# A fused attention and gated feed-forward kernel: two of the second layer's seven products split into seven smaller ones, with their sums on GpSimd, and results stored 32 rows at a time

## The chip, the cores and the metric

The kernel runs on one core of one Trainium2 chip. Such a core has five engines that run their own streams of instructions and meet only at semaphores: TensorE (PE in the profile; its weight loads are PEld), VectorE (DVE), ScalarE (ACT), GpSimd (POOL), and SyncE (SP), which here only issues transfers. TensorE writes to PSUM, the others work on SBUF, VectorE and ScalarE on PSUM too. Transfers to and from the device's memory run on 16 DMA engines. The metric is the device time of one execution in microseconds.

## The reference

Everything is float32. For each of 8 batches and 8 heads, with 576 rows of 64 columns:

```python
kv = np.einsum('bhsd,bhse->bhde', k, v)
out = np.einsum('bhsd,bhde->bhse', q, kv)
rms = np.sqrt(np.mean(out * out, axis=-1, keepdims=True) + 1e-06)
attn = out / rms * g_norm
```

The heads of one row are then put beside each other: `x` has 4608 rows and 512 columns, and goes through a gated feed-forward block with `w_gate` and `w_val` of 512 x 1536 and `w_out` of 1536 x 512:

```python
gate = 1.0 / (1.0 + np.exp(-(x @ w_gate)))
result = (gate * (x @ w_val)) @ w_out
```

The weights come as float64 and are converted on the chip.

## The kernel before

**Chunks.** The 4608 rows are worked on in nine chunks `c` of 512 rows (`G`), 0 to 8. A chunk goes through a first layer (`x` times the two wide weights, sigmoid, product: 12 tiles `gv` of 128 features by 512 rows) and a second layer (`gv` times `w_out`). Chunk 0 is computed plainly, while weights arrive and the attention of batches 0 and 1 is done. From chunk 1 on both layers use a scheme of Strassen's kind (Winograd's form): two by two blocks are multiplied with seven products in place of eight, at the price of sums of blocks. In the first layer one of those seven is itself split into seven again, with matmuls of 128 columns (`small`).

**The first layer** (`first_layer_fast`) runs over six pairs of features `f`. For each it issues TensorE's products in a fixed order, VectorE additions that collect them from PSUM, ScalarE copies and sigmoids in tiles `sg` (four buffers), and on GpSimd the sums of the next pair's weights (`w_sum`, `w_sums2`). After each pair VectorE forms the sums of `gv` that the second layer wants: `s12` and `s4` (`h_sum`, `h_sums`). The last pair of a chunk also issues the weight sums for the first pair of the next.

**The second layer** (`second_layer_fast`) takes two groups `g` of 2 x 128 rows. For each it runs seven products of six matmuls of 256 columns (line 870), in PSUM banks that it takes from a queue of five (`take`, `give`), and gathers the results in two `sg` tiles: `o2` for the rows of tile `2 + g`, `o1` for those of tile `g`. `t2w` are sums of blocks of `w_out`, formed once, during chunk 1. When both tiles of a group are complete they are stored. The order of the seven is: `gv` low times `b[1,1]`, `s12` times `t2w[2]`, `gv` high times `b[2,1]`, `gv` low times `t2w[3]`, `s12` times `t2w[1]`, `gv` high times `t2w[4]`, `s4` times `b[2,2]`. A matmul call of float32 is two instructions in the profile, so a product shows as x12.

**Order.** Nothing is reordered by a planner: every engine gets its instructions in the order in which the program writes them. What isn't part of the layers is put into a queue `fill`, and `slot()` takes one step out of it: seven times for each pair of features in the first layer, twice for each product in the second, so 42 and 28 times a chunk. In chunks 1 to 6, `feed(c + 1)` provides the attention steps of batch `c + 1`: transposes of q on VectorE (`turn`), k^T v on TensorE (`kv_mm`) and its copies on ScalarE (`kv_copies`), then, for two pairs of heads at a time (`two_pairs`), q times k^T v on TensorE, square and root on ScalarE, sums, scaling and transposes on VectorE, and transfers of the transposed result into the next chunk's `xT` through SP. Steps called `idle` do nothing but take a slot. After them come the sums of the next chunk's rows (`x_sums`, eight VectorE operations).

**Transfers.** SP issues nearly all of them, in order: k and v of the batch after next (`load_late`, at the end of a second layer, into the 21 buffers that `gv`, `s12` and `s4` also rotate through), q after the second transpose of a pair, the transfers into `xT`, and the stores. From batch 2 on, the rows of `x` lie in an order in which 32 rows of a tile are rows of the output six apart; `store` (line 487 on) writes one, two or three such groups in one DMA. Only the last two stores, of half a tile each, also use ScalarE's queue.

Of the kernel before, what the change touches and what calls it, by code (L numbers as in the profile page):

```python
# [20 lines left out]
def kernel(  # L21
# [11 lines left out]
    nc = tc.nc  # L33
# [71 lines left out]
    def load_late(b):  # L105


        if b >= B:
            return
        mains = {}  # L110
        for n in range(NHP):
            for name, src in (("k", k), ("v", v)):
                mains[n, name] = t = hp.tile([P, G], FP32, tag="gv", name="kv")
                nc.sync.dma_start(out=t.rearrange("p (h c) -> p h c", h=2),
                                  in_=src[b, 2 * n:2 * n + 2, 0:S4].rearrange("h (p j) d -> p h (j d)", j=NK4))
        rest = hp.tile([P, G], FP32, tag="gv", name="kv")
        for i, src in enumerate((k, v)):
            for r in range(2):
                nc.sync.dma_start(out=rest[PH * r:PH * r + PH, GH * i:GH * i + GH].rearrange("p (h d) -> p h d", d=HD),
                                  in_=src[b, NHP * r:NHP * r + NHP, S4:S].rearrange("h p d -> p h d"))  # L120
        kv_late[b] = mains, rest
# [219 lines left out]
    def feed(b):  # L341
# [96 lines left out]
        def turns_of(n):  # L438
            return [(DVE, lambda n=n, e=e: turn(n, e)) for e in range(2)]
# [2 lines left out]
        steps = turns_of(n0)  # L442

        if b > 2:
            steps += [(PE, idle)] * 4
        steps.append((PE, kv_mm))
        for i in range(2 * NC):
            for rs in ((0, 1), (2,)):
# [2 lines left out]
        u, *rest = two_pairs(n0)  # L451
        steps += turns_of(n0 + 1) + [u] + rest[:1] + [(PE, idle)] * (3 if b > 2 else 0) + turns_of(n0 + 2) + rest[1:]

        steps += [(PE, idle)] + turns_of(n0 + 3) + [(PE, idle)] * (4 if b > 2 else 0)
        return steps + two_pairs(n0 + 2) + [(PE, idle)] * 4

    def idle():
# [20 lines left out]
        return gv[c, f]  # L478

    def sg_tile():  # L480
        return sb.tile([P, G], FP32, tag="sg", name="sg", bufs=4)

    def store(c, t, ot, cols=slice(0, DM), queues=(nc.sync,)):

        r0 = i = 0
        while r0 < P:
            b, s = divmod(G * c + P * t + r0, S)
            rows = out[S * b:S * b + S, cols]
            if b < 2:
                j, p = divmod(s, NP)  # L490
                n = min(P - r0, NP - p)
                queues[i % len(queues)].dma_start(out=rows.rearrange("(p j) d -> j p d", j=NJ)[j, p:p + n],
                                                  in_=ot[r0:r0 + n, cols])
            else:
                half, c0 = divmod(s, S // 2)
                r, c0 = divmod(c0, XC)
                n = min(P - r0, XC - c0)
                queues[i % len(queues)].dma_start(
                    out=rows.rearrange("(r p g i) d -> i r g p d", p=QB, g=JH, i=2)[half, r, c0 // QB:(c0 + n) // QB],
                    in_=ot[r0:r0 + n, cols])  # L500
            r0 += n
            i += 1
# [28 lines left out]
    def give(i):  # L531
        free.append(i)
# [190 lines left out]
    def first_layer_fast(c):  # L723
        s, a, s2, ax = sx[c], quarters(c), sx2[c], quarters(c)[1, 2]

        def product(ps, wt, xs, new):
            for m in range(NK):
                nc.tensor.matmul(ps, wt[:, m, :], xs[:, m, :], start=(new and m == 0), stop=(m == NK - 1),  # L728
                                 skip_group_check=True)

        def small(ps, wt, xs, new):
            nc.tensor.matmul(ps, wt, xs, start=new, stop=True, skip_group_check=True)  # L732


        def p1(d):
            d["ia"], d["pa"] = take()
            product(d["pa"], d["bg"][:, 0:NK], a[1, 1], True)
            d["u"] = d["sg"] = sg_tile()
            nc.scalar.copy(out=d["sg"][:, h2], in_=d["pa"])  # L739

# [34 lines left out]
        for f in range(NF2):  # L775
# [3 lines left out]
            ones, twos = one["bg"], two["bg"]  # L779

            p1(one)
            p1(two)
            slot()


            g1, g2 = one["sg"], two["sg"]
            i_d = free[2]
            del free[2]
            pd = bank(i_d)
            small(pd[:, q1], ones[:, NK], ax[:, 0, q1], True)  # L790
            nc.scalar.copy(out=g1[:, q1], in_=pd[:, q1])
            small(one["pa"][:, q1], ones[:, NK + 1], ax[:, 1, q1], False)
            p6(one)
            small(pd[:, q1], tw2[2], s2[:, 1], False)
# [54 lines left out]
    def h_sums(c, f):  # L849
# [5 lines left out]
        tt(out=one[:, h2], in0=one[:, h1], in1=one[:, h2], op=ALU.subtract)  # L855
        tt(out=s4[c, f], in0=two[:, h1], in1=s[:, h2], op=ALU.subtract)

    def second_layer_fast(c):
        b = {(j, n): w2[:, NF2 * (j - 1):NF2 * j, DH * (n - 1):DH * n] for j in (1, 2) for n in (1, 2)}
        d1, d2 = slice(0, DH), slice(DH, DM)  # L860
        for g in range(2):
            t1, t2 = slice(P * g, P * g + P), slice(GH + P * g, GH + P * g + P)
            (i_a, pa), (i_b, pb) = (take() for _ in range(2))

            last = (c, g) == (NG - 1, 1)
            parts = [slice(0, DH // 2), slice(DH // 2, DH)] if last else [slice(0, DH)]

            def product(ps, hs, ws, new):
# [37 lines left out]
                    store(c, g, o1, y, (nc.sync, nc.scalar))  # L906
            if not last:
                store(c, g, o1)
            if g == 1:
                load_late(c + 2)  # L910

    def sums_of(c):
        if c < NG:
# [33 lines left out]
    for c in range(1, NG):  # L947
        if c + 1 < B:
            steps = feed(c + 1)
            if c == 1:  # L950

                i = 4
                while w2_sums:
                    steps.insert(i, (DVE, w2_sums.popleft()))
                    i += 3
            spread(steps, (1, 2, 3, 4, 5) if c == 1 else (2, 3, 4, 5))
        first_layer_fast(c)
        sums_of(c + 1)
        second_layer_fast(c)
        flush()  # L960


# [28 lines left out]
```

## Time and profile before

| what | value |
|---|---|
| median of 10 runs | 1076.39 us (1075.49 to 1079.07) |
| the profiled execution | 1075.69 us, span 1073.9 us, TensorE clock 0.998 |
| first layer, chunks 2 to 6 (first to last matmul) | 76.6 to 76.9 us |
| second layer, chunks 2 to 6 | 38.5 us |
| first and second layer, chunk 7 (no attention beside them) | 71.7 and 36.4 us |
| from the last matmul's stretch to the end | 8.0 us |

The span reaches from the first to the last instruction of the profiled execution. "Idle" of an engine is named after what ended it. A matmul's recorded duration includes time in which the next one has begun, so TensorE's rate is read from the starts. The tables by stretches give, for each engine, busy microseconds and (x) the number of instructions.

### The profile page before, as it was taken

To read this page: it belongs to the slowest core of one execution; us is meant where nothing else is said; L and a number is where in the kernel's file an instruction comes from. 1 tells how busy PE (TensorE), PEld (TensorE's weight loads), DVE (VectorE), ACT (ScalarE), POOL (GpSimd) and SP (SyncE) were. 2 spreads that over 40 slices of the span, in tenths; PEclk is the share of its full clock that TensorE was granted. 3 is DMA by queue.
4 is the path that set the end of the run, shared out by engine and by line. 5 is a ranking of instruction groups with operands and counts; after the bars stand their busy time and mean duration, and the time that the engine had idled before them with its cause. 6 is when DMAs were issued, how large, how long until landed. Compare 5 with 4: busy or idle time off the path is not lost.

```text
span 1073.9 us, 19464 instructions
## 1 busy us (share of the span) xinstructions
PE 1062.8 (99%) x7514; PEld 883.0 (82%) x7514; DVE 712.0 (66%) x1461; ACT 308.8 (29%) x737; POOL 442.1 (41%) x630
## 2 busy tenths in 40 slices
PE   9999999999999999999999999999999999999996
PEld 8544448888888888888888888888888888888886
DVE  4897767894579547863778357945786388628841
ACT  4654323331243114320423134312431122112210
POOL 0000036870367216640666046713663077307700
PEclk9999999999999999999999999999999999999999
DMA  9944710002400141012301140014001200010001
GB/s 266 247 157 157 244 31 20 24 18 59 119 12 15 44 128 33 12 35 64 98 23 35 43 119 13 25 46 137 13 12 27 58 2 1 2 38 2 1 1 40
DMA packets 69115, 64.96 MB, mean 60 GB/s; under 512 B 23712, under 2 KB 63008, under 8 KB 69024
## 3 DMA queue, kind: packets, MB, share of 16 engines
q1 hardware_dynamic: 68768, 63.69, 21.2%
q8 instruction: 60, 0.98, 0.4%
q14 instruction: 31, 0.25, 0.1%
q10 hardware_dynamic: 256, 0.03, 0.1%
HBM read 47.19 MB, written 9.44 MB: 53 GB/s over the span
## 4 chain that ended last, share of the span: by engine, by line
PE 97%; DMA 1%; DVE 1%; SPq 0%; issue 0%; DVEq 0%
PE mm L728 46%; PE mm L870 27%; PE mm L732 7%; PE mm L556 7%; PE mm L653 4%; PE at L395 2%; PE at L354 1%; DMA v<-in_v_dram 1%; PE at L556 1%; PE two L261 0%; PE two L291 0%; PE two L318 0%; PE two L272 0%; DMA g_col<-in_g_norm_dram 0%; PE at L360 0%; PE mm L634 0%
## 5 line engine op out<-in xcount | busy, mean ns | idle before, releaser
L720 POOL TENSOR_TENSOR tw<-gv 128x256 f32<-128x256 f32 x192 | 156.1, 823 | 231.6 <-DVE w L202 144.5
L728 PE MATMUL mm<-xT,tw 128*128 128x256 f32 x768 | 198.4, 381 | 0.0
L728 PE MATMUL mm<-sx,tw 128*128 128x256 f32 x768 | 197.4, 380 | 0.0
L802 POOL TENSOR_TENSOR sg<-sg 128x256 f32<-128x256 f32 x48 | 35.6, 742 | 341.5 <-ACT sg L801 341.3
L720 POOL TENSOR_TENSOR tw<-gv,tw 128x256 f32<-128x256 f32 x192 | 154.9, 826 | 0.0
L728 PEld LDWEIGHTS mm<-xT,tw 128*128 128x128 f32 x768 | 137.3, 190 | 17.4 <-issue 2.8
L728 PEld LDWEIGHTS mm<-sx,tw 128*128 128x128 f32 x768 | 134.9, 191 | 12.4
L773 DVE TENSOR_TENSOR gv<-gv,sg 128x256 f32<-128x256 f32 x192 | 108.4, 584 | 0.0
L728 PE MATMUL mm<-sx,gv 128*128 128x256 f32 x384 | 91.2, 380 | 0.0
L728 PE MATMUL mm<-xT,gv 128*128 128x256 f32 x384 | 90.8, 379 | 0.0
L870 PE MATMUL mm<-w,gv 128*128 128x256 f32 x384 | 89.1, 381 | 0.7 <-DVE gv L773 0.7
L870 PE MATMUL mm<-t2w,gv 128*128 128x256 f32 x384 | 88.7, 381 | 0.0
L870 PE MATMUL mm<-w,s 128*128 128x256 f32 (+1 forms) x408 | 88.3, 367 | 0.0
L764 ACT ACTIVATE sg<-sg 128x256 f32<-128x256 f32 x96 | 40.0, 416 | 151.1 <-DVE sg L763 150.9
L739 ACT COPY sg<-mm 128x256 f32<-128x256 f32 x96 | 35.8, 373 | 162.7 <-PE mm L728 160.9
L870 PEld LDWEIGHTS mm<-w,gv 128*128 128x128 f32 x384 | 72.5, 190 | 12.2 <-DVE gv L773 2.6
L870 PEld LDWEIGHTS mm<-w,s 128*128 128x128 f32 x408 | 74.1, 190 | 9.4
L728 PEld LDWEIGHTS mm<-xT,gv 128*128 128x128 f32 x384 | 72.9, 190 | 10.4 <-issue 0.5
L728 PEld LDWEIGHTS mm<-sx,gv 128*128 128x128 f32 x384 | 72.5, 190 | 10.0
L870 PEld LDWEIGHTS mm<-t2w,gv 128*128 128x128 f32 x384 | 72.4, 190 | 10.0
L556 PE MATMUL mm<-xT,gv 128*128 128x512 f32 x176 | 77.4, 593 | 0.0
L745 DVE TENSOR_TENSOR gv<-mm,sg 128x256 f32<-128x256 f32 x96 | 37.1, 414 | 41.3 <-PE mm L728 38.6
(120 smaller groups left out, 1550.4 us busy)
## 6 DMA issues: line engine op xcount, KB each, us to landing
q<-in_q_dram SPq DMA_DIRECT2D x24, 288.0 KB
st<-in_moe_w_gate_dram SPq DMA_DIRECT2D x12, 512.0 KB
st<-in_moe_w_val_dram SPq DMA_DIRECT2D x12, 512.0 KB
st<-in_moe_w_out_dram SPq DMA_DIRECT2D x12, 512.0 KB
kv<-in_k_dram SPq DMA_DIRECT2D x24, 256.0 KB
kv<-in_v_dram SPq DMA_DIRECT2D x24, 256.0 KB
out_dram<-sg SPq DMA_DIRECT2D x23, 192.0 KB
xT<-xTs SPq DMA_DIRECT2D x48, 72.0 KB
```

Of the source, the lines that this page charges most:

```text
L395: nc.tensor.matmul(u[HD * e:HD * e + HD, r, o:o + HD], qTs[QB * r:QB * r + QB, (n0 + which) % 2, c:c + PH], kvq[QB * r:QB * r + QB, (n0 + ...
L556: nc.tensor.matmul(self.ps[i], w[("wg", "wv")[i], self.f][:, m, :], xT[self.c][:, m, :], start=(m == 0), stop=(m == NMT - 1), skip_group_c ...
L653: nc.tensor.matmul(ps[t], gv[0, f][:, P * t:P * t + P], w["wo", f], start=(f == 0), stop=(f == NFT - 1), skip_group_check=True)
L720: nc.gpsimd.tensor_tensor(out=tw[f, i], in0=b[in0], in1=b[in1] if isinstance(in1, tuple) else tw[f, in1], op=ALU.subtract)
L728: nc.tensor.matmul(ps, wt[:, m, :], xs[:, m, :], start=(new and m == 0), stop=(m == NK - 1), skip_group_check=True)
L732: nc.tensor.matmul(ps, wt, xs, start=new, stop=True, skip_group_check=True)
L739: nc.scalar.copy(out=d["sg"][:, h2], in_=d["pa"])
L745: tt(out=d["h"][:, h1], in0=d["pb"], in1=d["sg"][:, h2], op=ALU.add)
L764: nc.scalar.activation(out=d["sg"][:, h2], in_=d["sg"][:, h2], func=AF.Sigmoid)
L773: tt(out=d["h"][:, h], in0=d["h"][:, h], in1=d["sg"][:, h], op=ALU.mult)
L802: nc.gpsimd.tensor_tensor(out=g2[:, h1], in0=g2[:, h1], in1=g2[:, h2], op=ALU.add)
L870: nc.tensor.matmul(ps, hs(f), ws[:, f, :], start=(new and f == 0), stop=(f == NF2 - 1), skip_group_check=True)
```

## The change

The second layer of chunks 1 to 7 is written anew; chunk 8 keeps the old order, now called `second_layer_last`.

- Both groups `g` now run through the first five products side by side (`gv` low times `b[1,1]`, `s12` times `t2w[2]`, `gv` low times `t2w[3]`, `s12` times `t2w[1]`, `s4` times `b[2,2]`), and four result tiles are filled at the same time. Between them GpSimd gets four sets of twelve additions of 128 x 128 (`sums2`), written over parts of `gv` and `s12` that TensorE has read by then.
- The two products left, `gv` high times `t2w[4]` and `gv` high times `b[2,1]`, are each taken for both groups at once, as a product of two by two blocks of 128 rows by 128 columns, with seven products of three matmuls of 128 columns (`split`). Each of the seven is added to the results at once.
- `sg` gets a fifth buffer. In the first layer the copy of the second gate (`p1_out(two)`) is issued after the first small product's copy.
- The results of the first split are stored between the splits and within the second, the others at the end.
- In `feed`, k^T v has six `idle` steps before it in place of four, and the second two pairs two in place of four. In chunk 1 the sums for `t2w` take every second place among the steps in place of every third.
- `store` writes 32 rows in each DMA for batches from 2 on.

The core of the diff (unchanged lines, index helpers and asserts are left out):

```diff
-            steps += [(PE, idle)] * 4
+            steps += [(PE, idle)] * 6
...
-        steps += [(PE, idle)] + turns_of(n0 + 3) + [(PE, idle)] * (4 if b > 2 else 0)
+        steps += [(PE, idle)] + turns_of(n0 + 3) + [(PE, idle)] * (2 if b > 2 else 0)
...
-        return sb.tile([P, G], FP32, tag="sg", name="sg", bufs=4)
+        return sb.tile([P, G], FP32, tag="sg", name="sg", bufs=5)
...
-                n = min(P - r0, XC - c0)
+                n = QB
                 queues[i % len(queues)].dma_start(
-                    out=rows.rearrange("(r p g i) d -> i r g p d", p=QB, g=JH, i=2)[half, r, c0 // QB:(c0 + n) // QB],
+                    out=rows.rearrange("(r p g i) d -> i r g p d", p=QB, g=JH, i=2)[half, r, c0 // QB],
                     in_=ot[r0:r0 + n, cols])
...
             p1(one)
+            p1_out(one)
             p1(two)
             slot()
...
             small(pd[:, q1], ones[:, NK], ax[:, 0, q1], True)
+            g1 = one["sg"]
             nc.scalar.copy(out=g1[:, q1], in_=pd[:, q1])
+
+            p1_out(two)
+            g2 = two["sg"]
...
+    def sums2(x, out, weights):
+        o = dict(zip((1, 2, 4, 3), out))
+        if weights:
+            ops = ((1, (1, 2), (1, 1)), (2, (2, 2), 1), (4, (2, 1), 2), (3, (2, 2), (1, 2)))
+        else:
+            o[3] = x[2, 1]
+            ops = ((1, (2, 1), (2, 2)), (2, 1, (1, 1)), (3, (1, 1), (2, 1)), (4, (1, 2), 2))
+        for i, in0, in1 in ops:
+            for j in range(N3):
+                u0, u1 = (x[n][j] if isinstance(n, tuple) else o[n][j] for n in (in0, in1))
+                nc.gpsimd.tensor_tensor(out=o[i][j], in0=u0, in1=u1,
+                                        op=ALU.add if i == 1 and not weights else ALU.subtract)
+        return o
...
+        for g in pair:
+            i_, pa = take()
+            product(pa, of(gv, lo, g), b[1, 1], True)
+            o2[g] = sg_tile()
+            nc.scalar.copy(out=o2[g][:, d1], in_=pa)
+            give(i_)
+        tw4 = sums2(b4, thirds(of(gv, lo, 0) + of(gv, lo, 1)), True)
+        for g in pair:
+            i_b[g], pb[g] = take()
+            product(pb[g], of(s12, lo, 2 + g), t2w[2], True)
+            o1[g] = sg_tile()
+            nc.scalar.copy(out=o1[g][:, d1], in_=o2[g][:, d1])
+            tt(out=o1[g][:, d2], in0=pb[g], in1=o2[g][:, d1], op=ALU.add)
+        sa4 = sums2(a4, thirds(of(s12, lo, 2) + of(s12, lo, 3))[:3], False)
+        for g in pair:
+            product(pb[g], of(gv, lo, 2 + g), t2w[3], False)
+            tt(out=o2[g][:, d1], in0=pb[g], in1=o2[g][:, d1], op=ALU.add)
+            give(i_b[g])
+        sa2 = sums2(a2, thirds(of(gv, lo, 2) + of(gv, lo, 3))[:3], False)
+        for g in pair:
+            i_c[g], pc[g] = take()
+            product(pc[g], of(s12, lo, g), t2w[1], True)
+            tt(out=o2[g][:, d2], in0=pc[g], in1=o2[g][:, d1], op=ALU.add)
+        tw2_ = sums2(b2, thirds(of(s12, lo, 0) + of(s12, lo, 1)), True)
+        for g in pair:
+            product(pc[g], of(s4, lo, g), b[2, 2], False)
+            tt(out=o1[g][:, d2], in0=pc[g], in1=o1[g][:, d2], op=ALU.add)
+            give(i_c[g])
+
+        def split(o, x, a, sa, w_, tw_, done=None):
...
+            small(pd, a[1, 1], w_[1, 1], True)
+            add(o[0][:, l], pd)
+            small(pf, a[1, 2], w_[2, 1], True)
+            add(o[0][:, l], pf)
+            slot()
+            small(pd, sa[2], tw_[2], False)
+            add(o[0][:, r], pd)
+            small(pe, sa[1], tw_[1], True)
+            add(o[1][:, r], pe)
+            slot()
+            small(pd, sa[3], tw_[3], False)
+            y = o[1][:, x].rearrange("p (n c) -> p n c", n=2)
+            tt(out=y, in0=y, in1=pd.unsqueeze(1).to_broadcast([P, 2, P]), op=ALU.add)
+            small(ph, a[2, 2], tw_[4], True)
+            add(o[1][:, l], ph)
+            slot()
+            if done:
+                done()
+            small(pe, sa[4], w_[2, 2], False)
+            add(o[0][:, r], pe)
+            slot()
...
+        split(o2, d1, a4, sa4, b4, tw4)
+        store(c, 2, o2[0])
+        split(o1, d1, a2, sa2, b2, tw2_, lambda: store(c, 3, o2[1]))
+        for g in pair:
+            store(c, g, o1[g])
+        load_late(c + 2)
...
-                    i += 3
+                    i += 2
...
-        second_layer_fast(c)
+        (second_layer_fast if c < NG - 1 else second_layer_last)(c)
```

Here `small` in `split` is three matmuls of 128 columns, `add` a VectorE addition of PSUM onto the result, `lo` and `hi` the six lower and six upper `gv` tiles, and `product` still calls `slot()` after every third matmul.

## The prediction

> **What bounds the kernel now.** I read the page first: busy shares, then the chain that ended last. TensorE is busy for 99% of the span and carries 97% of the chain, so a change counts by the TensorE time it takes away, by the stalls it puts into TensorE's order, and by what follows the last matmul.
>
> ```profile
> PE 1062.8 (99%) x7514; PEld 883.0 (82%) x7514; DVE 712.0 (66%) x1461; ACT 308.8 (29%) x737; POOL 442.1 (41%) x630
> PE 97%; DMA 1%; DVE 1%; SPq 0%; issue 0%; DVEq 0%
> ```
>
> Then the busy time by stretches: a second layer with attention steps (chunk 5), one without (chunk 7), the last one, and what follows it.
>
> ```profile
> core 0: us, PE busy (x) PEld busy (x) DVE busy (x) ACT busy (x) POOL busy (x), PEclk, DMA share, GB/s
> 697.00:735.30 38.30, 38.30 (x313) 33.40 (x312) 16.96 (x36) 4.21 (x7) 4.24 (x6) 1.00 0.18 48
> 921.50:957.80 36.30, 36.30 (x170) 31.96 (x169) 11.82 (x24) 1.49 (x4) 4.45 (x6) 1.00 0.07 16
> 1029.30:1065.90 36.60, 36.50 (x193) 32.59 (x191) 6.77 (x19) 1.49 (x4) 0.00 (x0) 1.00 0.08 21
> 1065.90:1073.90 8.00, 0.00 (x0) 0.00 (x0) 0.23 (x1) 0.00 (x0) 0.00 (x0) 0.75 0.19 38
> ```
>
> A second layer is solid matmul, with GpSimd idle after 4.5 us. The span ends with 8.0 us without matmuls, in which 0.19 of 16 DMA engines, three, are busy. Busy means of matmuls overlap, so I price TensorE by starts in the timeline, and take GpSimd's price from its own line:
>
> ```profile
> 714.39 2.75 PE L870 MATMUL mm<-w,s 128*128 128x256 f32 x12
> 716.98 2.75 PE L870 MATMUL mm<-w,gv 128*128 128x256 f32 x12
> ...
> 1057.69 2.84 PE L870 MATMUL mm<-w,s 128*128 128x128 f32 x24
> 1060.37 1.89 PE L870 MATMUL mm<-t2w,gv 128*128 128x256 f32 x8
> ...
> L713 POOL TENSOR_TENSOR tx<-gv,tx x96: 454/519/788, 153.8 to 1017.0; 128x128 f32<-128x128 f32 x96
> ```
>
> One call is two instructions. 256 columns cost (716.98-714.39)/12 = 215.8 ns each, 128 columns (1060.37-1057.69)/24 = 111.7 ns: half the columns cost 52%. The GpSimd line gives min/median/max in ns.
>
> Who waits says how the span ends and what holds the k, v loads:
>
> ```profile
> SPq L986 <- DMA out_dram<-sg: 5.6, 1, 5.6
> SPq L114 <- DMA out_dram<-sg: 10.0, 6, 3.0
> DVE sx L691 <- DMA xT<-xTs: 12.3, 6, 3.9
> ```
>
> After its last issue SP waits 5.6 us for a store to land; in six stages the loads queue behind stores, for up to 3.0 us.
>
> [...] the last store, written as [3 groups, 32 rows], issued at 1066.16, shows one jump at 1067.27 and then three counts, the last at 1072.59, while a one-group store issued at 1063.62 has 16 counts up to 1065.22 (1.6 us). [...] the same h sum takes 0.94 us beside GpSimd and 0.41 us after it. [...]
>
> **The change, part by part.**
>
> 1. *TensorE.* In chunks 1 to 7, four product calls (two products for both groups) of 6 matmuls of 256 columns go: 48 instructions x 215.8 = 10.36 us. Two splits of 7 x 3 matmuls of 128 columns come: 84 x 111.7 = 9.38 us. Gain 0.98 a chunk, x 7 = 6.8 us.
>
> 2. *GpSimd sums.* 4 x 12 = 48 additions of 128x128 a chunk, priced from the row above: 0.45 us alone, 0.64 as the bad end (the row of the fourth of those sums has a median of 636 ns, beside VectorE). They begin 4.5 us into the stage, when the old weight sums are done. Each set also waits for the tiles that it overwrites. In a stage with attention, TensorE's steps end at: first products 5.5 us, second 12.5 (with 1.7 us of attention), third 17.7, fourth 22.9, fifth 28.2; then the splits, 4.7 us each. At 0.45 the four sets end near 9.9, 15.4, 20.8 and 26.2; at 0.64 at 12.2, 19.9, 27.5 and 35.2. The first split wants its last sum at 32.2, the second at 35.7. So nothing at either end; the cover is five products of TensorE work. Without it, all 22 to 31 us would be on the path. In chunk 7 (no attention, wanted at 34.0) the bad end stalls 1.2 us once. I take 0.
>
> 3. *VectorE in the splits.* Fourteen additions of about 0.28 us replace four of 0.42. The third and fifth products of a split accumulate into the bank that an addition has just read, with one product (6 x 111.7 = 0.67 us) between. In the trace an addition starts 0.2 us after the next matmul's start, lasts 0.28, and a released weight load starts 0.05 after it: 0.53, against 0.56, when that load would start anyway. With an x sum of the next chunk before it (0.69 us; by my count of slots two such fall into the first split of chunks 2 to 6) it is 0.1 to 0.2 late. Bounds: 0 to about 0.5 for each of six waits a chunk. I take 0.25 us a chunk, 1.7 in all. New waits of TensorE's sequencer cost some 0.03 to 0.05 each (a weight load with a separate wait instruction, 51 ns, delays its matmul that much); 0.1 a chunk, 0.7. Behind a waiting matmul stands everything on TensorE.
>
> 4. *Steps moved.* k^T v and its eight ScalarE copies come two slots later, the first attention pair two to five, the second pair one slot earlier. That puts 1.1 us more of VectorE work into the last block of the first layer, which has 0.75 us of idle behind it; so VectorE enters the second layer some 0.3 us late. The first product's last pair of matmuls already waits for VectorE there (2.74 us instead of 2.59 for that product), so this lands on TensorE: 0.3 x 5 chunks (2 to 6) = 1.5 us. Bounds: 0 to 0.8 each. For chunk 1 the weight sums of the second layer only change places: I take 0, within 1 us. The ScalarE copy of the second gate moves behind another copy, 0.4 us later; its VectorE reader comes 1.9 us after: nothing.
>
> 5. *Fifth buffer.* Four results are now held at once. The next block's second gate takes the buffer of the first store; that store is issued after the first split and has 6.9 us to land, wanting 4 x 0.48 + 2 plus 0.5. Nothing.
>
> 6. *Stores.* Every tile of the later batches leaves in four DMAs of 32 rows, 0.43 us each on SP, instead of two of 0.43 to 0.80. At a stage's end eight stand before the k, v loads, 3.9 us instead of two at 1.2; but the 3.0 us wait on landings goes, and k^T v comes 2.6 us later. Nothing. In the tail: SP issues from 1063.6; four for the last full tile until 1065.5, two for the next half until 1066.5, two for the last half, the latter starting at 1067.0 and landing 1.6 to 2.4 us later, near 1069.0, where it is 1072.6 now. ScalarE's share ends sooner. Gain 3.6; bounds 2.5 to 4.4.
>
> Sum: -6.8 + 1.7 + 0.7 + 1.5 - 3.6 = -6.5 us. The profiled execution took 1075.7 with a span of 1073.9; so 1067.4 of span and 1069.2 for such an execution. The median shown is 0.7 above it: **1069.9**.
>
> **Rivals.**
>
> *All of the gain.* No stall of parts 3 and 4: -6.8 - 3.6 = -10.4, 1066.0. For it: bank hand-overs just fit. Against it: the first product shows that VectorE is already late.
>
> *Only the tail.* Stalls in the splits eat the TensorE gain of 0.98 a chunk: -3.6, 1072.8. For it: the gain is small, and VectorE is busy with sums in just that place. Against: of the eight x sums only two long ones fall inside.
>
> *Nothing comes of it.* The final wait hangs on issue or receipt rather than on three engines, and half of the TensorE gain is stalled away: about -1, 1075.4. Against: the 0.19 DMA share.
>
> *Slower: sums late.* The sums' own price on GpSimd is above its row, because blocking by VectorE or waits between them stretch each. The second split has its last sum in time up to (35.7-4.5)/48 = 0.65 us a step; each further 0.02 costs 1 us a chunk. The gain of 6.5 is gone at about 0.67. At 0.75: 40.5-35.7 = 4.8 x 6, and 6.5 in chunk 7, is 35 us, +29, 1105. For it: GpSimd's contended steps reach 0.64, and it has no slack after its 48. Against: in these stages VectorE mostly reads PSUM.
>
> **How the numbers follow.** My forecast 0.48 (1067.5 to 1072), all of the gain 0.17, only the tail 0.17, nothing 0.06, slower 0.12. About 0.2%, 2.2 us, is what a measurement of this kernel can tell: the first three are faster (0.82), the fourth the same (0.06), the last slower (0.12). The range leaves out the slow case and the edge of the best: 1065.5 to 1075.5.
>
> **What would show it.** Chunk 5's second layer at some 38.2 us from first to last matmul (now 38.5), chunk 7's at 35.8 (36.4); GpSimd with 48 more steps there at 0.45 to 0.55 us, done before the second split; no TensorE wait on GpSimd; small waits on VectorE at the split's accumulations; the tail at 4 to 5 us with many more engines busy. Wrong if TensorE shows long waits for GpSimd or for VectorE's additions, if k^T v waits for loads, or if the tail stays at 8 us.

## The result, and the profile after

The changed kernel takes 1067.19 us (median, 1066.56 to 1069.29), measured beside 1076.35 us for the kernel before: ratio 0.9916, 95% interval 0.9908 to 0.9925, so 9.2 us less. The profiled execution has a span of 1065.1 us, 8.8 less than before.

The page's busy shares and the chain that ended last, as they are now:

```profile
PE 1057.7 (99%) x7766; PEld 887.6 (83%) x7766; DVE 740.9 (70%) x1545; ACT 307.2 (29%) x737; POOL 587.5 (55%) x966
PE 98%; DMA 0%; SPq 0%; issue 0%; ACT 0%; DVE 0%
```

TensorE has 252 instructions more (7 chunks x 36) and is busy 5.1 us less; GpSimd has 336 more (7 x 48) and 145 us more, none of which enters the chain.

The busy time by stretches: the second layer of chunk 5, that of chunk 7, the last one, and what follows it (columns as in the head line):

```profile
core 0: us, PE busy (x) PEld busy (x) DVE busy (x) ACT busy (x) POOL busy (x), PEclk, DMA share, GB/s
694.77:732.25 37.48, 37.48 (x349) 33.81 (x348) 21.13 (x49) 4.07 (x7) 24.61 (x54) 1.00 0.21 52
917.85:953.25 35.40, 35.40 (x205) 32.29 (x204) 17.06 (x37) 1.35 (x4) 26.62 (x54) 1.00 0.06 14
1024.84:1061.40 36.56, 36.56 (x193) 32.69 (x191) 6.80 (x19) 1.49 (x4) 0.00 (x0) 1.00 0.10 24
1061.40:1065.10 3.70, 0.04 (x1) 0.00 (x0) 0.29 (x1) 0.00 (x0) 0.00 (x0) 0.79 0.22 53
```

A second layer is 0.8 us shorter, with attention or without, when it is taken from its first matmul to the next stage's first; the last, whose code is the old one, is the same; the end without matmuls went from 8.0 to 3.7 us.

The timeline of chunk 5's second layer (start, duration, engine and line, out<-in, number of instructions):

```profile
694.77 5.43 PE L894 MATMUL mm<-w,gv 128*128 128x256 f32 x24
...
699.13 1.64 POOL L883 TENSOR_TENSOR gv<-t2w 128x128 f32<-128x128 f32 x3
...
707.14 5.34 PE L894 MATMUL mm<-t2w,gv 128*128 128x256 f32 x24
...
709.42 4.99 POOL L883 TENSOR_TENSOR gv<-gv 128x128 f32<-128x128 f32 x12
...
718.10 1.27 POOL L883 TENSOR_TENSOR s<-w 128x128 f32<-128x128 f32 x3
...
722.68 1.50 PE L953 MATMUL mm<-t2w,gv 128*128 128x128 f32 x12
...
732.31 1.03 PE L729 MATMUL mm<-xT,gv 128*128 128x256 f32 x4
```

GpSimd's last new sum ends at 719.4, 24.6 us into the stage, before the first split has even begun (27.9). Twelve of its additions take 4.99 us, 0.42 each. The two splits take 732.31 - 722.68 = 9.63 us, 0.25 more than 84 x 111.7 ns.

GpSimd's line of the commonest of these sums (min/median/max in ns, records that overlap the next one a little), and all that TensorE waits for in the whole execution (us in total, times, longest):

```profile
L883 POOL TENSOR_TENSOR gv<-gv x105: 442/446/467, 249.2 to 939.1; 128x128 f32<-128x128 f32 x105
...
PE at L395 <- issue: 1.6, 2, 0.9
PE mm L635 <- POOL ident masks.py:199: 1.4, 1, 1.4
PE two L291 <- ACT qTs L277: 0.6, 2, 0.3
```

There is no wait for GpSimd's sums; the one for `ident` is at the kernel's start. The 0.7 us that TensorE waited for VectorE's `gv` in chunk 1 of before is gone. New is the first line: twice 0.7 to 0.9 us inside the 144 small matmuls of q times k^T v (line 395), for nothing that the profile shows. It comes up again below.

SP's waits for stores, before 10.0 us ahead of the k, v loads and 5.6 us at the end, are now one:

```profile
SPq L1118 <- DMA out_dram<-sg: 1.1, 1, 1.1
```

Where the 8.8 us of span come from, stage by stage (first matmul to the next stage's first, before to after; "ideal" counts TensorE's instructions at 215.8 and 111.7 ns):

| part | predicted | in the traces |
|---|---|---|
| TensorE work of the seven second layers | -6.8 | -6.9 (ideal) |
| waits inside them, splits included | +2.4 | +1.3: 0.18 a chunk (38.34 to 37.55 us; 36.26 to 35.44 in chunk 7) |
| first product's wait for VectorE | +1.5 | -0.9: nothing added in chunks 2 to 6, chunk 1's of 0.9 gone |
| first layers, and the start of chunk 1 | 0 | +2.0: chunk 2 +0.85, chunk 4 +0.93, chunk 5 -0.35, the rest +0.6 |
| from the last second layer's start to the end | -3.6 | -4.5: 44.7 to 40.2 us |
| sum | -6.5 | -8.8 (the parts are rounded) |

The first product by itself takes 12 x 0.2158 = 2.59 us where nothing holds it up. In chunks 2 to 6 it took 2.74 to 2.75 us before and takes 2.67 now; in chunk 1 it took 3.57 and takes 2.62.

### The profile page after: what moved, and what is told of

Read it like the earlier page. It is cut to its first block, busy times and chain, and to the rows that moved or that the text cites. A ratio compares the mean times of both kernels' runs of the same rounds, so it can differ in the third digit from the quotient of the medians.

```text
span 1065.1 us, 20718 instructions
## 1 busy us (share of the span) xinstructions
PE 1057.7 (99%) x7766; PEld 887.6 (83%) x7766; DVE 740.9 (70%) x1545; ACT 307.2 (29%) x737; POOL 587.5 (55%) x966
## 4 chain that ended last, share of the span: by engine, by line
PE 98%; DMA 0%; SPq 0%; issue 0%; ACT 0%; DVE 0%
PE mm L729 47%; PE mm L894 17%; PE mm L557 7%; PE mm L733 7%; PE mm L953 6%; PE mm L654 4%; PE mm L1004 3%; PE at L395 2%; PE at L354 1%; PE at L557 1%; DMA q<-in_q_dram 0%; PE two L291 0%; PE two L261 0%; PE mm L635 0%; PE two L318 0%; PE two L272 0%
## 5 line engine op out<-in xcount | busy, mean ns | idle before, releaser
L721 POOL TENSOR_TENSOR tw<-gv 128x256 f32<-128x256 f32 x192 | 158.6, 836 | 257.2 <-DVE w L202 144.9
L776 DVE TENSOR_TENSOR gv<-gv,sg 128x256 f32<-128x256 f32 x192 | 110.8, 596 | 0.0
L729 PEld LDWEIGHTS mm<-xT,gv 128*128 128x128 f32 x384 | 72.3, 190 | 10.0 <-issue 0.5
L894 PE MATMUL mm<-w,s 128*128 128x256 f32 x336 | 73.7, 379 | 0.0
L894 PEld LDWEIGHTS mm<-w,s 128*128 128x128 f32 x336 | 63.8, 190 | 8.7
L752 DVE TENSOR_TENSOR gv<-mm,sg 128x256 f32<-128x256 f32 x96 | 40.0, 417 | 40.5 <-PE mm L729 39.5
L557 PEld LDWEIGHTS mm<-xT,gv 128*128 128x128 f32 x176 | 32.6, 190 | 37.4 <-issue 35.9
L766 DVE TENSOR_TENSOR sg<-mm,sg 128x256 f32<-128x256 f32 x96 | 40.4, 421 | 33.0 <-PE mm L729 32.9
L748 DVE TENSOR_TENSOR gv<-mm,sg 128x256 f32<-128x256 f32 x96 | 36.6, 413 | 37.6 <-PE mm L729 37.6
L714 POOL TENSOR_TENSOR tx<-gv,tx 128x128 f32<-128x128 f32 x96 | 54.6, 569 | 7.5
```

The lines of the kernel that those rows point to most:

```text
L557: nc.tensor.matmul(self.ps[i], w[("wg", "wv")[i], self.f][:, m, :], xT[self.c][:, m, :], start=(m == 0), stop=(m == NMT - 1), skip_group_c ...
L714: nc.gpsimd.tensor_tensor(out=tw2[i], in0=in0, in1=tw2[in1] if isinstance(in1, int) else in1, op=ALU.subtract)
L721: nc.gpsimd.tensor_tensor(out=tw[f, i], in0=b[in0], in1=b[in1] if isinstance(in1, tuple) else tw[f, in1], op=ALU.subtract)
L752: tt(out=d["h"][:, h2], in0=ps, in1=d.pop("u")[:, h2], op=ALU.add)
L766: tt(out=d["sg"][:, h2], in0=d["pb"], in1=d["sg"][:, h2], op=ALU.add)
L776: tt(out=d["h"][:, h], in0=d["h"][:, h], in1=d["sg"][:, h], op=ALU.mult)
```

## The experiments

**The stores alone.** The kernel before with the 32-row stores only.

```diff
-                n = min(P - r0, XC - c0)
+                n = QB
...
-                    out=rows.rearrange(...)[half, r, c0 // QB:(c0 + n) // QB],
+                    out=rows.rearrange(...)[half, r, c0 // QB],
```

> The kernel before with nothing but the stores of 32 rows. Theory (three DMA engines carry the last stores): only the tail moves, from 8.1 us after the last second-layer matmul to 3.6, so 4.5 us less than before, near 1071.9, and every stage up to there is the same within 0.3 us. Rival (the tail hangs on issue and receipt): no more than 1 us less. Rival (eight more issues on SP hold the k, v loads back): waits of TensorE for k, v appear in the first layers and the time is 1076 or more.

Measured: 1071.89 us, ratio 0.9964 (0.9957 to 0.9971) to before, 4.3 us less. Its stretches at the end:

```profile
1030.39:1067.00 36.61, 36.61 (x193) 32.69 (x191) 6.81 (x19) 1.49 (x4) 0.00 (x0) 1.00 0.10 24
1067.00:1071.00 4.00, 0.00 (x0) 0.00 (x0) 0.29 (x1) 0.00 (x0) 0.00 (x0) 0.75 0.21 50
```

The tail falls from 8.0 to 4.0 us, and the stages of chunks 1 to 7 before it stay within about 0.3 us. In the kernel before, the old stores ahead of the k, v loads cost nothing.

**The old stores in the changed kernel.** The same edit undone.

```diff
-                n = QB
+                n = min(P - r0, XC - c0)
...
-                    out=rows.rearrange(...)[half, r, c0 // QB],
+                    out=rows.rearrange(...)[half, r, c0 // QB:(c0 + n) // QB],
```

> The changed kernel with the stores of up to 96 rows as before. Theory: the stages of the changed kernel stay, the tail is 8.1 us again: 4.5 us more than the changed kernel, near 1071.7. Rival (the small stores also free the loads or the result buffers in the middle of the kernel): more than 5.5 us above the changed kernel, with waits of ScalarE for buffers or of TensorE for k, v.

Measured: 1075.44 us, ratio 0.9990 (0.9983 to 0.9997): 8.3 us worse than the changed kernel, of which the tail explains 4.2. The theory missed the other 4.1, which are what the expectation's rival described. In the profiled execution, which took 1.5 us more than the median, three first layers are longer than in the changed kernel's: chunk 3's by 1.4 us, chunk 5's by 3.8, chunk 6's by 0.8. Its waits, and its timeline where chunk 5's first layer begins (619.65):

```profile
ACT sg L742 <- DMA out_dram<-sg: 6.0, 6, 2.6
PE mm L733 <- ACT sg L802: 1.6, 2, 1.1
PE at L354 <- DMA kv<-in_v_dram: 1.3, 2, 0.7
```

```profile
620.78 4.59 SPq L499 DMA_DIRECT2D out_dram<-sg  x3
...
625.47 1.51 SPq L114 DMA_DIRECT2D kv<-in_k_dram  x1
...
635.53 0.37 SPq L114 DMA_DIRECT2D kv<-in_v_dram  x1
...
640.06 0.69 PE L354 MATMUL at<-kv 128*64 128x64 f32 x16 [0.73 <-DMA kv<-in_v_dram]
641.28 0.58 PEld L354 LDWEIGHTS at<-kv 128*64 128x64 f32 x16 [0.68 <-DMA kv<-in_k_dram]
641.32 0.69 PE L354 MATMUL at<-kv 128*64 128x64 f32 x16 [0.57 <-DMA kv<-in_v_dram]
```

Two things happen when the old stores meet the new order. The ScalarE copy of the second gate (line 742) waits for its buffer up to 2.6 us, and TensorE for the copies behind it. And three stores hold SP for 4.59 us, the k, v loads leave behind them, some as late as 16 us into the stage, and k^T v, which begins at 18.5, finds its data missing. In the changed kernel the last k, v load of the same stage has landed 14.6 us into it. So the 32-row stores are no side change: the new order of results needs them. Which part of the new order does it, four results held at once or more stores close to the stage's end, was not tried apart.

**The two products whole.** The new order, four results, moved steps and stores as they are; the two split products are taken whole, without GpSimd's sums.

```diff
-        tw4 = sums2(b4, ...)          # and the three other sets
...
-        split(o2, d1, a4, sa4, b4, tw4)
-        store(c, 2, o2[0])
-        split(o1, d1, a2, sa2, b2, tw2_, lambda: store(c, 3, o2[1]))
+        for g in pair:
+            i_, pa = take()
+            product(pa, of(gv, hi, 2 + g), t2w[4], True)
+            tt(out=o2[g][:, d1], in0=pa, in1=o2[g][:, d1], op=ALU.add)
+            give(i_)
+            store(c, 2 + g, o2[g])
+        # the same for gv high times b[2, 1] into o1[g]
```

> The changed kernel with the two split products taken whole again (six matmuls of 256 columns for each group, no sums on GpSimd), everything else in the new order. Theory (the split gives 0.98 us a chunk of matmul time less 0.18 of small waits): second layers of chunks 2 to 6 at about 38.3 us where the changed kernel has 37.55, 0.8 x 7 = 5.6 us more than the changed kernel, near 1072.8. Rival (the new order, with VectorE relieved, earned the gain and the split nothing): the same as the changed kernel within 1 us. Rival (the sums cost time elsewhere by blocking VectorE): 3 to 4 us more, with first layers shorter.

Measured: 1072.20 us, ratio 0.9968 (0.9956 to 0.9980), 5.0 above the changed kernel. Its second layers of chunks 2, 3, 5 and 6 last 38.26 to 38.27 us, chunk 7's 36.26. Against 37.55 and 35.44 the split is worth 0.7 and 0.8 us a chunk, out of the 0.98 of instructions: 5.0 of the 9.2 us in all. The rest is about what the stores gain alone (4.3). Nothing else of the new order makes a second layer shorter, but chunk 1 here too lacks the wait of before (38.40 us, not 39.17). Chunk 4's second layer is left out of this comparison: it lasts 39.18 us, with a stop that is looked at below.

**The attention steps where they were.** The changed kernel with before's idle steps.

```diff
-            steps += [(PE, idle)] * 6
+            steps += [(PE, idle)] * 4
...
-... turns_of(n0 + 3) + [(PE, idle)] * (2 if b > 2 else 0)
+... turns_of(n0 + 3) + [(PE, idle)] * (4 if b > 2 else 0)
```

> The changed kernel with the idle steps of the attention as before (4 and 4 in place of 6 and 2). Theory: k^T v comes 2.6 us sooner, 16.4 us into the first layer, and k, v of chunk 5 had landed at 15.5, so TensorE doesn't wait for them; the time is within 1.5 us of the changed kernel, and what moves comes from gaps inside the bursts of small matmuls of the attention (0.9 us in chunk 2 and 1.2 in chunk 4 of the changed kernel, just after a 16 KB instruction fetch), which fall elsewhere when the bursts move: 1065 to 1068.5. Rival (the two slots are needed): TensorE waits for k, v by 0.5 to 3 us in each of five chunks: 1070 to 1080.

Measured: 1065.47 us (1064.40 to 1065.84), ratio 0.9898 (0.9883 to 0.9913), so 1.7 us below the changed kernel; the span is 1062.6, 2.5 less. k^T v waits for no load. The second layers of chunks 2 to 6 last 37.61 us in place of 37.55: moving the steps neither cost nor gave more than 0.06 us there. The difference lies in the first layers of chunks 2 and 4 (77.27 and 77.55 us in the changed kernel, 76.25 here), and TensorE's waits have lost the line `at L395 <- issue`.

**What stops the small matmuls.** This is how such a stop looks in the changed kernel, in chunk 2's first layer (timeline; in brackets, idle time before and what ended it), and the line of the queue that the page calls `q8 instruction` (packets, MB, share):

```profile
319.76 1.70 PE L395 MATMUL at<-kvq,qTs 32*64 32x64 f32 x136
...
322.12 0.34 PE L395 MATMUL at<-kvq,qTs 32*64 32x64 f32 x8 [0.67 <-issue]
```

```profile
q8 instruction: 62, 1.02, 0.4%
```

Those 62 transfers are of 16,384 bytes, about 1.1 us each. The kernel before has 60 of them and 504 TensorE records less (matmuls and weight loads, 15,028 against 15,532): about 250 records to a transfer in both, from which I estimate that the queue is TensorE's. The 144 matmuls and their 144 weight loads, 288 instructions in 1.73 us where nothing stops them, are the densest stretch that TensorE has; elsewhere 1.73 us of the trace hold at most 132. In the trace one such transfer starts at 319.4, 0.34 us before this burst; the other stopped burst, at 548.5, starts 0.03 us after one. If the stops go with the transfers, moving the bursts against the transfers moves the stops. The two kernels below put n small matmuls, into a bank that nobody reads, ahead of chunk 1, with n = 18 and 38:

```diff
+    i_, pa = take()
+    for _ in range(18):
+        nc.tensor.matmul(pa[0:PH, 0:PH], ident[0:QB, 0:PH], ident[0:QB, 0:PH], start=True, stop=True)
+    give(i_)
     for c in range(1, NG):
```

> The changed kernel with 18 idle matmuls of 64 columns before chunk 1, 72 instructions in TensorE's stream, which nothing reads; everything after them is the same. Theory [...]: by the positions of the fetches in the changed kernel's profile no burst falls on a fetch any more, so the 0.9 us gap in chunk 2 and the 1.2 us gap in chunk 4 go and 0.4 us come for the padding: 1.7 us less than the changed kernel, near 1065.5, and no gap over 0.2 us. Rival (the gaps come from the work in those chunks): 0.4 us more, 1067.6, with the gaps in the same bursts.

> The same with 38 idle matmuls, 152 instructions. Theory [...]: up to five of the twelve bursts now begin where a fetch does, 0.9 us each, in place of the two of the changed kernel: 2 to 3 us more and 0.9 for the padding, 1068.5 to 1071, with gaps in other chunks than 2 and 4. Rival (the gaps belong to chunks 2 and 4): 0.9 us more, 1068.1, with the gaps where they were.

Measured: 1069.36 us for 18 (ratio 0.9942, 0.9929 to 0.9956) and 1073.08 for 38 (0.9966, 0.9951 to 0.9982). Both totals are above their forecasts, because the padding itself was dearer: 2.2 and 5.5 us where it stands, and 0.5 and 2.4 more in chunk 1's first layer. With 38 the trace has the reason. These are the stretches of the padding and of what follows it (columns as before; the third value from the end is the granted clock):

```profile
159.47:164.98 5.51, 5.51 (x77) 5.39 (x76) 0.00 (x0) 0.59 (x1) 0.00 (x0) 0.81 0.31 90
164.98:168.50 3.52, 3.52 (x9) 2.86 (x9) 0.00 (x0) 0.37 (x1) 0.00 (x0) 0.50 0.00 0
```

The profile shows TensorE busy throughout, and yet its granted clock falls to 0.50: chunk 1's first eight matmul instructions take 3.78 us in place of 1.89. With 18 the clock stays at 1.00; of the 0.5 us, 0.3 are a stop behind a burst in chunk 1, and the rest stays open.

The stops moved: with 18, those of chunks 2 and 4 are gone and a new one is in chunk 5, in a burst that begins 0.31 us after a transfer's start; with 38 there is none inside a burst, where I had counted on up to five, since the transfers had moved too. Over all 156 such bursts in the traces of before, after and the eleven experiments:

```
burst begins after the start of an instruction transfer    bursts    first matmul to the next product's, us
0.03 to 0.36 us                                                14    2.34 to 2.91
0.93 to 1.18 us                                                 8    1.73 to 2.11
later                                                         134    1.73 to 1.92
```

Outside the first row no burst is stopped for more than 0.4 us within it, and none in the first row escapes. The 14 are not 14 independent cases: six of the kernels have the same TensorE matmuls, and 12 of the 14 are the same two bursts in them (chunks 2 and 4). Counting each burst of a program once, there are 72, and the first row has four.

Nor does the table show every stop. A few come just behind a burst, in the next matmuls of 256 columns. This is the one in chunk 4 of the run with whole products:

```profile
588.81 1.80 PE L395 MATMUL at<-kvq,qTs 32*64 32x64 f32 x144
592.75 2.86 PE L894 MATMUL mm<-t2w,s 128*128 128x256 f32 x12 [0.65 <-issue]
```

It costs 0.8 us; three more, of 0.2 to 0.7 us, are in the two kernels with padding, one of them in chunk 2's second layer with 18. In these four cases the last transfer had begun 18 to 21 us before the burst and the next began 0.3 to 1.9 us after its start, but other bursts placed like that were not stopped. So the stops inside a burst went with the place of the transfers wherever the bursts were moved. That the transfers cause them was not shown: the records show a coincidence in time, and what decides on the stops behind a burst stays open.

**How much room GpSimd has.** Each addition of the first two sets once more (24 a chunk), or of all four sets (48), written to a spare tile that nobody reads.

```diff
+                if again:
+                    nc.gpsimd.tensor_tensor(out=spare, in0=u0, in1=x[1, 1][j], op=ALU.subtract)
```

> The changed kernel with 72 GpSimd additions a chunk in place of 48 (those of the first two sets each once more, into a spare tile that nobody reads). Theory: the 48 end 24.6 us into a second layer of chunk 5, one takes 0.42 us there, so 72 end near 34.7, and the second split wants its last sum at 35.5 (37.55 less three small products of 0.69): no wait, the time of the changed kernel within 1 us, 1066.2 to 1068.2. Rival (GpSimd's share already costs time through VectorE's blocked additions): 24 more steps add 0.5 us a chunk or more, 1071 and above.

> The changed kernel with every one of the 48 additions issued once more into a spare tile, 96 a chunk. Theory (a deadline that 72 just meet): they end near 4.4 + 96 x 0.42 = 44.7 us into a second layer, 9.2 us after the second split wants the last, 11.3 in chunk 7: 6 x 9.2 + 11.3 = 66 us more than the changed kernel, near 1133, with TensorE waiting for GpSimd in the splits. Rival (the price of a step falls or its order hides more): less than 1110. Rival [...]: above 1145.

Measured with 24 more: 1074.27 us, ratio 0.9982 (0.9976 to 0.9989); 7.1 above the changed kernel, so most of its gain on before is gone. GpSimd ends 36.7 us into the stage; the second split's fifth product, which takes the last sums, begins at 35.5 in the changed kernel. Second layers are 0.8 us longer, chunk 7's 2.6. My expectation of no change had taken the steps at their undisturbed 0.42 us; the third set took 0.54 a step (chunk 5), beside VectorE's sums of the next rows (0.76 to 0.86 us each there, in place of 0.68; the first of them once 1.26 and once 1.67 in other chunks).

With 48 more (one execution): 1182.59 us, some 50 more than the theory; of the two rivals, the one above 1145 is nearer. GpSimd ends 44 to 46 us into the stage, but the stages last 48.6 to 56.8. What TensorE waits for, and the timeline of chunk 5 in that run:

```profile
PE mm L957 <- DVE sg L961: 76.2, 6, 16.6
PE mm L957 <- POOL s L885: 8.2, 2, 7.0
```

```profile
797.55 11.54 DVE L695 TENSOR_TENSOR sx<-xT,sx 128x512 f32<-128x512 f32 x1
...
806.86 0.45 POOL L885 TENSOR_TENSOR s<-w 128x128 f32<-128x128 f32 x1
807.27 0.45 POOL L888 TENSOR_TENSOR spare<-w 128x128 f32<-128x128 f32 x1
...
810.77 5.39 PE L957 MATMUL mm<-s,gv 128*128 128x128 f32 x24 [9.30 <-DVE sg L961]
```

A VectorE sum of two SBUF tiles, 0.68 us in the changed kernel, lasts 11.54 us while GpSimd runs its additions one after the other, each at its usual 0.45. Behind it in VectorE's order stand the additions that free TensorE's banks. And after that idle time TensorE's 24 matmul instructions take 5.39 us in place of 2.9. In chunks 3 and 6 the first of the sums lasted still longer (chunk 3):

```profile
524.03 18.75 DVE L692 TENSOR_TENSOR sx<-xT 128x512 f32<-128x512 f32 x1
```

To tell apart what VectorE and what TensorE's slow rate cost, the next run has the same 48 extra additions, but ScalarE copies one input where VectorE formed the eight sums of the next rows, so that the sums themselves are left out (the first of the eight is shown):

```diff
-            lambda: tt(out=s[:, 0], in0=a[2, 1], in1=a[2, 2], op=ALU.add),
+            lambda: nc.scalar.copy(out=s[:, 0], in_=a[2, 1]),
```

> The kernel with 48 additions more on GpSimd per second layer (they write a tile nobody reads), and the eight sums of the next chunk's rows replaced by one-input copies of the same tiles on ScalarE, so that the next first layer works on numbers that are not the sums. Theory: in the run with 48 more additions it was VectorE's two-input sums, held up beside an unbroken stream of GpSimd additions, that stopped TensorE, in order ahead of the additions it waits for. Then the second layers are bounded by GpSimd's own end, 44 to 46 us into the stage, plus about 2 us: 46 to 48 us instead of 49 to 57, and the run ends at about 1125 to 1145. Rival: TensorE's slow rate after its idle time, or GpSimd's waits, made the time: 1165 to 1185 again.

Measured (one execution): 1136.18 us. The second layers last 46.6 to 47.0 us, and TensorE waits for GpSimd itself and no longer for VectorE:

```profile
PE mm L957 <- POOL s L885: 34.5, 21, 5.0
```

So the held-up VectorE sums, with what followed from them, made those 46 us. Which additions lose time beside GpSimd can be read in the changed kernel's trace: of the 48 of line 861, with both inputs from SBUF, 47 run wholly beside GpSimd and take 0.94 us (median), the one away from it 0.42; of the 96 of line 766, with one input from PSUM, 94 run beside it and 2 away from it, and the median is 0.42 for both. A sum that meets an unbroken row isn't always served after the next GpSimd addition: the 11.54 us span 26 starts of GpSimd additions, the 18.75 us 44, and both sums ended 0.55 us after the last addition of the row. That isn't always so: in chunk 5 of the same run three earlier sums were served within the row, the first of them after 4.56 us; in the run with 24 more, the same sums met a set of twelve additions and mostly took only 0.1 to 0.2 us longer, one GpSimd addition at a time giving way (0.9 us). What makes a row give way or not stays open. The slow matmuls after the pause are a part of the loss: in the stretch from 808 to 816.6 us TensorE's granted clock is 0.54. The run with copies is not free of them (0.50 from 524.6 to 531.4 us). What brings the clock down was not shown: it fell here around a pause of 9.30 us, and with 38 idle matmuls while TensorE was busy.

**Four buffers for results.**

```diff
-        return sb.tile([P, G], FP32, tag="sg", name="sg", bufs=5)
+        return sb.tile([P, G], FP32, tag="sg", name="sg", bufs=4)
```

> The changed kernel with four result buffers instead of five, everything else kept, the 32-row stores too. Theory: the fifth buffer is worth nothing once stores land fast. The next first layer's second gate takes the buffer that the first result of the second split leaves only with its store; with 32-row stores the four results are on their way within about 2 us of the stage's end and land 1.5 us after their issue, while that gate's copy is wanted about 2.6 us into the next first layer. Then 1067.2, within 0.5 us. Rival: the copy of that gate waits for the third and fourth store; ScalarE's waits for a landing at the sigmoid and copy lines would then show 0.5 to 2 us in each of six or seven stages, and the time would be 1069 to 1075.

Measured: 1066.67 us, ratio 0.9911 (0.9896 to 0.9926), the changed kernel's. (With four, the second gate's buffer is the one of `o2[1]`, not of a result of the second split, as I had written.) That gate's copy begins 2.31 us into the next first layer, as with five, and 2.41 once. The fifth buffer is worth nothing as long as stores land as fast as here (1.7 us after their issue at the median in the changed kernel).

**A version that beats both.** The attention steps where they were, and the last full tile's four stores on two queues.

```diff
-            store(c, 2 + g, o2)
+            store(c, 2 + g, o2, queues=(nc.sync, nc.scalar) if last else (nc.sync,))
```

> The changed kernel with before's idle steps in the attention order, and the four stores of the last full tile shared between SP's and ScalarE's queues. Theory: the idles of before cost nothing (1065.5, as measured for that edit alone), and SP, which issues 0.43 us per transfer up to 2.1 us after the last matmul, ends about 0.5 to 0.9 us earlier with two issues less: 1064.6 to 1065.0. Rival: the end is set by the last half tile's own additions, issue and landing (SP has waited for the addition anyway): 1065.5, no difference to that edit alone.

Measured: 1064.80 us (1064.54 to 1065.71), ratio 0.9895 (0.9879 to 0.9912): 11.0 us below before, 2.4 below the changed kernel. Most of this is the steps' place. How the changed kernel and this one end (timeline):

```profile
1059.25 3.65 SPq L499 DMA_DIRECT2D out_dram<-sg  x8
1060.14 0.29 DVE L1038 TENSOR_TENSOR sg<-mm,sg 128x128 f32<-128x128 f32 x1 [0.91 <-PE mm L1004]
1060.46 2.13 ACTq L499 DMA_DIRECT2D out_dram<-sg  x4
1061.48 0.29 DVE L1038 TENSOR_TENSOR sg<-mm,sg 128x128 f32<-128x128 f32 x1 [1.05 <-PE mm L1004]
```

```profile
1057.34 3.32 SPq L499 DMA_DIRECT2D out_dram<-sg  x6
1057.34 3.39 ACTq L499 DMA_DIRECT2D out_dram<-sg  x6
1058.22 0.29 DVE L1038 TENSOR_TENSOR sg<-mm,sg 128x128 f32<-128x128 f32 x1 [0.91 <-PE mm L1004]
1059.56 0.29 DVE L1038 TENSOR_TENSOR sg<-mm,sg 128x128 f32<-128x128 f32 x1 [1.05 <-PE mm L1004]
```

From the last addition's start to the end of SP's last issue it is 1.42 us there and 1.10 here; from the last second layer's start to the end of the span, 40.23 and 40.08 (40.26 with the moved steps alone put back). So at most 0.2 us was gained, less than the 0.5 to 0.9 expected: each queue still has two issues of the last half tile, which wait for that addition, and their landing. Whether sharing the queues is worth anything, the times can't tell (1064.80 against 1065.47, with spans of 1063.0 and 1062.6).

## Why the prediction was right, point by point

The forecast was 1069.9, the time is 1067.2: between the forecast and the rival "all of the gain" (1066.0), and nearer to the rival. It lies inside the range of 1065.5 to 1075.5, but 0.3 us below the band that had been called "my forecast" (from 1067.5), to which 0.48 was given.

1. *TensorE, -6.8.* Right. The split against the whole products shows 0.7 to 0.8 us of it a chunk, and the rest is in point 3.
2. *GpSimd sums, nothing.* Right, with more room than thought: 0.42 us a step and an end at 24.6 us, where 26.2 was worked out for the good end. In chunk 7, where VectorE's sums of the next rows meet the first set, that set takes 0.6 us a step, and the end is at 26.6. The rival "sums late" has its deadline at the right place (35.7, measured 35.5): an end at 36.7 us, forced by 24 more steps, costs most of the gain. What stood against that rival, that VectorE mostly reads PSUM here, holds: in chunk 7, from 929.56 us on, GpSimd's steps take 0.42 us, and VectorE's additions from PSUM beside them 0.42 too. What the rival had not seen is the way in which crowding GpSimd hurts most, by VectorE's sums.
3. *VectorE and the sequencer in the splits, +2.4.* The waits are there, the size was off: 0.25 us a chunk in the splits, where 0.35 was taken, and 0.18 more than before for the whole second layer, 1.3 in all. By the starts of the matmuls, 0.16 of the 0.25 are four delays of 0.04, before the third and the fifth product of each split; they are all that chunk 7 has, and a wait of 51 ns of TensorE's sequencer stands ahead of each, taken at 0.1 in all. Only 0.09 are VectorE, taken at 0.25: in chunk 5 the addition that frees the bank for the first split's fifth product stands behind a sum of the next rows and ends at 30.54 us into the stage, and the weight load begins at 30.66. No wait of the splits is long enough to be listed.
4. *Moved steps, +1.5.* Wrong. The step that fails is the 0.3 us by which VectorE should be late at the second layer's first product: that product became shorter, 2.67 us, and takes 2.74 again with the steps put back, which leaves the second layers of chunks 2 to 6 within 0.06 us. What the move did cost, 1.0 us in chunk 2 and 1.3 in chunk 4 against the kernel with the steps back, went with something else: the two stopped bursts, which began 0.34 and 0.03 us after the start of an instruction transfer (a coincidence, not a cause that was shown). In the chunk where I took 0, chunk 1, 0.9 us of waiting went. It went from the first product, so before the new order of the second layer begins; the weight sums' new places or the later copy of the second gate may have done it, which was not tried apart.
5. *Fifth buffer, nothing.* Right as it stands, and with four buffers too; with the old stores the copy waits up to 2.6 us.
6. *Stores: nothing in the middle, -3.6 in the tail.* The tail is the right place, mis-sized: -4.5, just past the bound of 4.4; alone, in the kernel before, -4.3. The last store of three groups landed 6.4 us after its issue (1066.16 to 1072.59); the last one of 32 rows took 1.5 us (1062.49 to 1063.97) and not 2.0, and its issue began a little earlier. That the number of engines makes this difference is an estimate from the DMA share of 0.19 before (0.22 in the tail now); it was not shown by itself. In the middle, "nothing" is right only together with the edit: the count of 3.9 us against 2.4 of issues looked at the price of the new stores, and not at what the old ones would have cost in the new order, 4.1 us more by the run with them.

That the sum came out within 2.7 us is in part luck. The prediction took too much time by 1.1 us in point 3, by 1.5 and 0.9 in point 4 and by 0.9 in the tail, 4.4 in all; 2.0 us in the start and the first layers, most of it the two stops, which no step had, took nearly half of that back. With the stops out of the way, as in the run with the steps put back, the time is 1065.47, at the very edge of the range.

## What to carry to other kernels

Price a stage against the deadline of each helper engine, and add what the helper does to a third engine whose instructions stand in order before the ones that the bottleneck waits for. Ask of every edit that seems a side change whether the main one could live without it: here the small stores hold up the new order as well as shortening the tail. And where a change has moved dense bursts of small instructions, look for stops named "issue" inside them and just behind them before giving the loss to a dependency; here, putting the bursts elsewhere by two steps cost nothing.

## What the runs showed of the hardware that was not expected

- A burst of 288 short TensorE instructions in 1.73 us took 0.6 to 1.2 us longer when it began within 0.36 us after the start of a 16,384-byte instruction transfer (14 of 14 executions, of four different bursts), and at most 0.4 us longer otherwise. Four times a stop of 0.2 to 0.8 us came just behind a burst instead.
- A VectorE addition of two SBUF tiles lasted up to 18.8 us beside an unbroken row of GpSimd additions, which kept on starting every 0.41 us, but mostly 0.76 to 0.86 us beside a shorter row. In the changed kernel the row has ended when they come, except in chunk 7 (chunk 5: last GpSimd sum at 719.4, first VectorE sum at 720.6), and they last 0.68; a few us more of GpSimd's work and they meet. In chunk 7 they meet the first set, and both sides give way: 0.83 to 0.94 us a VectorE sum, 0.6 a GpSimd step.
- TensorE's granted clock fell to 0.50 while the profile showed it busy throughout, with 76 matmul instructions of 32 rows by 64 columns in 5.5 us (0.81 on average there, 0.50 in the 3.5 us after them). With 36 of them, in 2.2 us, it stayed at 1.00.
